# Four units of W1: the low words brought down by ACT and added by POOL, where DVE shifted and merged them

## The chip, the core and the metric

The kernel runs on one core of one Trainium2 chip. The core has five engines with a queue each: TensorE (PE, matmuls, and PEld for its weight loads), VectorE (DVE), ScalarE (ACT), GpSimd (POOL) and SyncE (SP, which here issues the DMAs). Instructions of one engine run in the order of its queue, and wait for others by semaphores. The metric is the device time of one execution in microseconds, lower is better.

## The reference, cut to what matters

```python
def _attn_ref(q, k, v, phi):                    # 8 batches, 8 heads, 576 tokens, 64 wide, 32 memories
    a = softmax(phi, axis=2)                    # over tokens
    k_m = einsum('bhsm,bhsd->bhmd', a, k)
    v_m = einsum('bhsm,bhsd->bhmd', a, v)
    attn = softmax(q @ k_m.T / sqrt(64))
    return attn @ v_m
def _moe_ref(x, w_ch1, w_ch2):                  # x: 8 x 576 x 512
    u = x + real(fft(fft(x, axis=1), axis=2))
    un = (u - mean(u)) / sqrt(var(u) + 1e-6)    # over the 512
    return u + maximum(un @ w_ch1, 0) @ w_ch2   # 512 -> 2048 -> 512
```

The two weight matrices arrive in double precision, 64 bits an element. The kernel needs them in single precision, and makes that on the chip.

## The kernel before, in words

The 4608 tokens are 36 tiles of 128, two tiles a chunk, 18 chunks. For each batch the attention and the transform are made in the background (`background`), and each chunk goes through the two layers: `ffn1` writes hidden values to PSUM (`ph`), ACT applies ReLU, `ffn2` accumulates into `po`, and `finish` adds `u` and stores. W1 and W2 are cut into eight units each, unit j of W1 holding 256 of the 2048 hidden columns and unit j of W2 the matching rows. In this text "W1 unit 3" is that piece; in the code its key is `"1_3"`, and for W2 `"2_3"`.

Chunk 0 goes through the layers while the weights are still coming in, in single precision (`ffn1_direct`, L675, and `ffn2_direct`, L692). For unit j: `load_stage` (L761) brings 1 MB of 64-bit words into a staging place; `to_f32` makes the single-precision values; `ffn1_direct` uses W1 unit j in two halves, `ph_j_0` and `ph_j_1`, each followed by a ReLU on ACT (L678); `ffn2_direct` uses W2 unit j, again in two halves, each of which needs the ReLU of the same half. `split_w1` (L803 and L808, or L806) then makes the pairs of half-precision values with which all later chunks work. The staging places are few: the load of W1 unit 3 goes to the place of W1 unit 1, unit 4 to that of unit 2, unit 6 to that of unit 4, W2 unit 6 to that of W1 unit 5, W1 unit 7 in two halves (tiles `hring` and `uring`) to that of W2 unit 5. A place is free once the conversion has read it for the last time.

`to_f32` treats a 64-bit word as a high and a low word of 32 bits, side by side in the staging tile. For a unit of 128 x 1024 elements:

- L771, ACT: brings the high word, read as a float, into range and drops its sign.
- L773, DVE: shifts the result left by 3 bits, in place.
- L774, DVE: puts the sign back (two operands, the high words and the result).
- then the upper three bits of the low word are set in. For most units DVE does it in one step (L784: shift the low word right by 29 and OR it into the result). For the units in the list `LP`, all of W2, DVE shifts the low word in place (L779, needs nothing but the load) and POOL adds it to the result (L782).
- L793, ACT: sum of squares, from which the unit's scale is made.

The order in each engine's queue is set at build time by a scheduler that runs the program on its own model of time; it is not the order of the code. So a change to `to_f32` also moves instructions that it doesn't touch. Beside the conversions the queues hold, in this stretch, the last tiles of batch 0 (`pp_t`, `px_t` on PE; L600 on ACT; L603, L617 on DVE) and the start of batch 1: transposes of phi (`pf`, `pl`), DVE's reductions to a maximum (L293 to L297), ACT's exponentials (L301 and L302, four of them), the scaling (L311), transposes back (`pt_e`) and the copies to `et` (L315).

Of the kernel before, what the change touches and what calls it, by code (L numbers as in the profile page):

```python
# [15 lines left out]
AF = mybir.ActivationFunctionType  # L16
ALU = mybir.AluOpType
# [33 lines left out]
UW = UB * DM  # L51
EB = 14
L2 = [2, 4, 6]
LP = ["2_0", "2_2", "2_4", "2_6"]
W1_STAGE = ["w4", "w6", "s1", "w6", "s1", "s2", "s1", "x"]
W2_STAGE = ["b10", "b14", "s2", "b10", "b14", "x", "s2", "s1"]
# [75 lines left out]
def kernel(  # L132
# [10 lines left out]
    nc = tc.nc  # L143
# [56 lines left out]
    def tiny(tag, n, bufs=2):  # L200
        if tag not in rings:
            rings[tag] = [taken[0], 0]
            taken[0] += n * bufs
        o, i = rings[tag]
        rings[tag][1] += 1
        o += i % bufs * n
        assert taken[0] <= 400, taken
        return scratch[:, o : o + n]

    def all_sum(src, n, key, pt=None, c0=0):  # L210

        if pt is None:
            pt = psg.tile([P, 512], F32, tag="g", name=f"as_{key}")
        nc.tensor.matmul(pt[:, c0 : c0 + n], lhsT=ones, rhs=src, start=True, stop=True)
        return pt[:, c0 : c0 + n]
# [548 lines left out]
    def to_f32(stages, dst, key):  # L764

        n = UW // len(stages)
        for i, stage in enumerate(stages):
            wf = stage.rearrange("p (a b) -> p a b", b=2)
            hi, lo = wf[:, :, 1], wf[:, :, 0]
            part = dst[:, n * i : n * (i + 1)]  # L770
            nc.scalar.activation(part, hi.bitcast(F32), AF.Abs, scale=2.0**-112)  # L771
            d = part.bitcast(I32)
            nc.vector.tensor_scalar(out=d, in0=d, scalar1=3, scalar2=None, op0=ALU.logical_shift_left)  # L773
            marks[key] = nc.vector.scalar_tensor_tensor(  # L774
                out=d, in0=hi, scalar=-0x80000000, in1=d, op0=ALU.bitwise_and, op1=ALU.bitwise_or
            )
            lu = lo.bitcast(U32)
            if key in LP:
                marks[key] = nc.vector.tensor_scalar(  # L779
                    out=lu, in0=lu, scalar1=29, scalar2=None, op0=ALU.logical_shift_right  # L780
                )
                nc.gpsimd.tensor_tensor(out=d, in0=lo, in1=d, op=ALU.add)  # L782
            else:
                marks[key] = nc.vector.scalar_tensor_tensor(  # L784
                    out=part.bitcast(U32),
                    in0=lu,
                    scalar=29,
                    in1=part.bitcast(U32),
                    op0=ALU.logical_shift_right,
                    op1=ALU.bitwise_or,  # L790
                )
        sq = tiny("sq", 2, 4)
        marks["sq" + key] = nc.scalar.activation(elt.rearrange("p l c -> p (l c)").bitcast(BF16)[:, :UW], dst, AF.Square, accum_out=sq[:, 0:1])  # L793
        return all_sum(sq[:, 0:1], 1, f"sq_{key}")
# [4 lines left out]
    def split_w1(j):  # L799
# [3 lines left out]
        nc.scalar.activation(w[:, 0], src, AF.Copy, scale=s)  # L803
        if j in L2:
            nc.scalar.activation(src, src, AF.Copy, scale=s)
# [6 lines left out]
    def prepare_w1(j):  # L812

        t = w1_f32(j)
        top = to_f32(parts_w1.pop(j), t, f"1_{j}")
        s = s1[:, j : j + 1]
        norm_scale(s, is1[:, j : j + 1], top, 1, 9, f"w1_{j}")
# [4 lines left out]
    def stage_w2(j):  # L822
        top = to_f32(parts_w2.pop(j), w2_f32(j), f"2_{j}")
        norm_scale(s2[:, j : j + 1], is2[:, j : j + 1], top, 1, 14, f"w2_{j}")
# [8 lines left out]
    def prepare_w2():  # L833
        for j in range(NW):
# [3 lines left out]
            nc.scalar.activation(w[:, :, 0], t, AF.Copy, scale=s)  # L838
            if j in L2:
                nc.scalar.activation(t, t, AF.Copy, scale=s)  # L840
# [221 lines left out]
```

## Time and profile before

| | us |
|---|---|
| median of three runs | 996.77 (996.4 to 997.15) |
| the profiled execution | 996.51 |
| its span | 994.6 |
| PE busy, 0 to 65 | 42.47 of 65 |
| PE busy, 65 to 134 (chunk 0 through the layers) | 64.19 of 69 |
| PE busy, 134 to 210 | 68.87 of 76 |
| PE busy, 210 to the end | 780.24 of 784.6 |

The times are of one execution taken by the hardware profiler. Matmuls are pipelined and their ends are modelled. A row of a timeline merges neighbours in the queue of the same line; `xN` says how many, and the bracket behind it how long the engine stood idle before and what ended that. Rows of DVE overlap by some 0.08 us, since the next instruction starts while the last one writes out.

### The profile page before, as it was taken

The numbers are of one execution on the slowest core, as the hardware profiler recorded it, in microseconds if no ns is written. First come the engines' busy times: TensorE is split into PE (matmuls) and PEld (weight loads), VectorE is DVE, ScalarE is ACT, GpSimd is POOL, SyncE is SP. The second block draws the span as 40 slices with busy tenths as digits, with TensorE's granted clock in tenths as the row PEclk, the third lists the DMA queues.
The fourth block names the chain that finished last, engine by engine and source line by source line (L and its number), as shares of the span: only waits on it lengthen the run. The fifth ranks groups of instructions, "written<-read, shape, count | busy, mean of one in ns | idle before, by whom it ended". The sixth has DMA issues, their size and how long they took to land.

```text
span 994.6 us, 18638 instructions
## 1 busy us (share of the span) xinstructions
PE 955.8 (96%) x7644; PEld 685.8 (69%) x7644; DVE 568.1 (57%) x1287; ACT 456.3 (46%) x913; POOL 228.0 (23%) x249
## 2 busy tenths in 40 slices
PE   5769999899999999999999999999999999999998
PEld 5756678666677777767767767777777777766664
DVE  1689967867655575657532576657745676311111
ACT  2265557586535563655431555456545543411100
POOL 1122235235221241233120032113311241300000
PEclk9979999999999999999999999999999999999999
DMA  9706545064222641384210643164213411210000
GB/s 351 270 1 253 184 152 154 2 138 117 64 43 59 136 98 41 56 153 103 58 22 22 117 120 61 48 119 121 68 43 62 101 19 35 44 39 4 22 22 22
DMA packets 115957, 88.06 MB, mean 89 GB/s; under 512 B 100384, under 2 KB 100384, under 8 KB 113824
## 3 DMA queue, kind: packets, MB, share of 16 engines
q1 hardware_dynamic: 115872, 86.87, 34.6%
q8 instruction: 60, 0.98, 0.4%
q14 instruction: 25, 0.20, 0.1%
HBM read 58.15 MB, written 9.44 MB: 68 GB/s over the span
## 4 chain that ended last, share of the span: by engine, by line
PE 84%; DVE 9%; ACT 2%; DMA 2%; issue 1%; SPq 0%; POOL 0%; DVEq 0%; ACTq 0%; POOLq 0%
PE po L728 34%; PE ph L255 33%; PE pm L255 5%; PE pp_t L255 3%; PE psc L255 2%; PE px_t L255 1%; PE pa L548 1%; PE pv L521 1%; PE po L692 1%; DVE w1t L784 1%; DVE uring L617 1%; DVE w2s L774 1%; DMA et<-elt 1%; DMA uring<-in_w 1%; DMA rawt<-in_raw 1%
## 5 line engine op out<-in xcount | busy, mean ns | idle before, releaser
L255 PE MATMUL ph<-unring,w1t 128*128 128x256 f16 x3264 | 390.3, 273 | 2.4 <-DVE scratch L638 1.4
L728 PE MATMUL po<-w2s,hring 128*128 128x512 f16 x1632 | 381.1, 380 | 3.1 <-ACT w2s L838 1.8
L255 PEld LDWEIGHTS <-w1t 128*128 128x128 f16 x3264 | 316.0, 98 | 66.3 <-issue 2.6
L728 PEld LDWEIGHTS <-hring 128*128 128x128 f16 x1632 | 157.6, 98 | 161.5 <-issue 5.6
L719 DVE SCALAR_TENSOR_TENSOR hring<-ph,hring 128x512 f16<-128x512 f32 x136 | 93.3, 686 | 157.4 <-ACT hring L718 156.9
L718 ACT ACTIVATE hring<-ph 128x512 f16<-128x512 f32 x136 | 80.1, 589 | 167.7 <-PE ph L255 167.6
L456 POOL TENSOR_TENSOR aring<-aring,scratch 128x384 f32<-128x384 f32 x28 | 24.7, 882 | 186.6 <-DVE scratch L454 163.5
L641 POOL TENSOR_TENSOR scratch<-scratch,small 128x1 f32<-128x1 f32 x36 | 23.9, 679 | 165.6 <-DVE scratch L640 152.9
L255 PEld LDWEIGHTS <-stg 128*128 128x128 f16 x1152 | 46.1, 98 | 10.3 <-issue 1.7
L373 POOL TENSOR_TENSOR stg<-rawt,stg 128x640 f16<-128x640 f32 x12 | 17.6, 1464 | 122.4 <-ACT rawt L372 122.4
L662 POOL TENSOR_TENSOR ud<-un,ud 128x1024 f16<-128x1024 f32 x17 | 36.7, 2160 | 33.9 <-ACT ud L661 33.8
L255 PE MATMUL pm<-et,stg 128*128 128x64 f16 (+1 forms) x780 | 39.1, 203 | 2.0 <-DMA et<-elt 2.0
L440 DVE TENSOR_REDUCE scratch<-psc 128x12 f32<-128x384 f32 x32 | 17.8, 556 | 39.2 <-PE psc L255 39.1
L255 PE MATMUL pp_t<-vh,at 128*128 128x255 f16 (+3 forms) x288 | 36.7, 273 | 0.0
L603 DVE SCALAR_TENSOR_TENSOR share<-pp_t,scratch,small 128x257 f32<-128x257 f32 (+1 forms) x48 | 21.0, 479 | 26.6 <-ACT small L600 26.5
L740 DVE SCALAR_TENSOR_TENSOR uring<-po,small,uring 128x512 f32<-128x512 f32 x34 | 24.5, 744 | 19.2 <-PE po L728 19.2
L675 PE MATMUL ph<-unring,w1t 128*128 128x256 f32 x128 | 33.5, 409 | 2.0 <-DVE w1t L784 1.5
L475 ACT CAST aeo<-eo 128x384 f16<-128x384 f32 x30 | 15.3, 510 | 43.9 <-DVE eo L472 43.9
L450 ACT ACTIVATE aring<-aring,scratch 128x384 f32<-128x384 f32 x24 | 14.6, 610 | 45.0 <-DVE aring L449 45.0
L617 DVE SCALAR_TENSOR_TENSOR uring<-px_t,scratch,share 128x256 f32<-128x256 f32 (+1 forms) x80 | 33.9, 476 | 0.2
L692 PE MATMUL po<-w2s,hring 128*128 128x512 f32 x64 | 31.5, 621 | 2.4 <-ACT hring L678 2.4
L675 PEld LDWEIGHTS ph<-unring,w1t 128*128 128x128 f32 x128 | 26.0, 207 | 11.1 <-issue 4.6
(226 smaller groups left out, 1271.9 us busy)
## 6 DMA issues: line engine op xcount, KB each, us to landing
rawt<-in_raw SPq DMA_DIRECT2D x15, 640.0 KB, 5.6
stg<-in_raw SPq DMA_DIRECT2D x15, 640.0 KB, 5.1
out<-uring SPq DMA_DIRECT2D x36, 256.0 KB, 2.1
stg<-in_w SPq DMA_DIRECT2D x7, 1024.0 KB, 5.1
rawt<-in_raw SPq DMA_DIRECT2D x15, 384.0 KB, 3.2
stg<-in_raw SPq DMA_DIRECT2D x15, 384.0 KB, 3.2
phs<-in_raw SPq DMA_DIRECT2D x32, 160.0 KB, 5.2
w2s<-in_w SPq DMA_DIRECT2D x4, 1024.0 KB, 9.6
```

What stands on the lines that cost most here:

```text
L255: m = nc.tensor.matmul(out, lhsT=lhsT, rhs=rhs, start=start, stop=stop)
L456: eng.tensor_tensor(out=a, in0=a, in1=sm.unsqueeze(2).to_broadcast([P, 12, M]), op=ALU.mult)
L603: nc.vector.scalar_tensor_tensor(out=tm[rows, w * NJ : (w + 1) * NJ], in0=pp[rows, :NJ], scalar=beta[rows], in1=qs[rows], op0=ALU.mult, op ...
L617: nc.vector.scalar_tensor_tensor(out=u[rows, hs], in0=px[rows, hs], scalar=igx[rows], in1=tm[rows, w * NJ + half : w * NJ + half + 256], o ...
L641: nc.gpsimd.tensor_tensor(out=rs, in0=rs, in1=half, op=ALU.pow)
L662: marks[f"ul{c}"] = nc.gpsimd.tensor_tensor(out=ud[:, 1], in0=un, in1=ud[:, 0], op=ALU.subtract)
L675: nc.tensor.matmul(ph, lhsT=w[:, k, f * P : (f + 1) * P], rhs=unTs[0][:, k], start=(k == 0), stop=(k == NK - 1))
L692: nc.tensor.matmul(po[t], lhsT=h[:, f, t], rhs=w[:, f], start=(j == 0 and f == 0), stop=(j == NW - 1 and f == UB - 1),)
L718: nc.scalar.activation(h[:, 0], phv, AF.Relu)
L719: nc.vector.scalar_tensor_tensor(out=h[:, 1], in0=phv, scalar=0.0, in1=h[:, 0], op0=ALU.max, op1=ALU.subtract)
L728: nc.tensor.matmul(po[t], lhsT=hs[j][:, lh, f * 2 + t], rhs=w2s[:, j * UB + f, lw, :], start=(j == 0 and f == 0 and i == 0), stop=(j == NW ...
L740: nc.vector.scalar_tensor_tensor(out=u, in0=po[t], scalar=cout if c else 0.5, in1=u, op0=ALU.mult, op1=ALU.add)
```

## The change

A new list `LA` names four units of W1. For them L784 is replaced: an activation on ACT reads the low word as an unsigned integer, multiplies it by 2^-29 and writes it back in place as a signed integer; POOL adds it to the result. W1 unit 7 is staged in two places, so it has two activations and two adds of half the size. Lines behind it move down by 1 to 4.

```diff
 L2 = [2, 4, 6]
+LA = ["1_1", "1_3", "1_5", "1_7"]
 LP = ["2_0", "2_2", "2_4", "2_6"]
...
             lu = lo.bitcast(U32)
-            if key in LP:
+            if key in LA:
+                nc.scalar.activation(lo, lu, AF.Copy, scale=2.0**-29)
+                nc.gpsimd.tensor_tensor(out=d, in0=lo, in1=d, op=ALU.add)
+            elif key in LP:
                 marks[key] = nc.vector.tensor_scalar(
                     out=lu, in0=lu, scalar1=29, scalar2=None, op0=ALU.logical_shift_right
                 )
                 nc.gpsimd.tensor_tensor(out=d, in0=lo, in1=d, op=ALU.add)
             else:
```

The queue of ACT in the middle of the stretch, before. `w1t<-stg` is L771 of W1 unit 6, `ph_j_f` (with a buffer number behind) is half f of unit j, whose ReLU it is, and `phs` are the exponentials of batch 1.

```order
L678 ACTIVATE hring<-ph_3_1_801 128x256
L771 ACTIVATE w1t<-stg 128x1024
L678 ACTIVATE hring<-ph_4_0_875 128x256
L678 ACTIVATE hring<-ph_4_1_881 128x256
L678 ACTIVATE hring<-ph_5_0_958 128x256
L301 ACTIVATE phs,scratch<-pf_0_647,scratch 128x512
L302 ACTIVATE phs,scratch<-pl_646,scratch 128x64
L301 ACTIVATE phs,scratch<-pf_1_654,scratch 128x512
L302 ACTIVATE phs,scratch<-pl_646,scratch 128x64
```

The same place now (lines of the changed kernel: L679 is the ReLU, L772 the old L771, L780 the new activation, L302 and L303 the exponentials; `w1t<-hring` is the first half of W1 unit 7).

```order
L772 ACTIVATE w1t<-stg 128x1024
L679 ACTIVATE hring<-ph_3_1_803 128x256
L679 ACTIVATE hring<-ph_4_0_877 128x256
L772 ACTIVATE w2s<-stg 128x1024
L302 ACTIVATE phs,scratch<-pf_0_648,scratch 128x512
L303 ACTIVATE phs,scratch<-pl_647,scratch 128x64
L302 ACTIVATE phs,scratch<-pf_1_655,scratch 128x512
L303 ACTIVATE phs,scratch<-pl_647,scratch 128x64
L679 ACTIVATE hring<-ph_4_1_883 128x256
L772 ACTIVATE w1t<-hring 128x512
L780 ACTIVATE hring<-hring 128x512
L679 ACTIVATE hring<-ph_5_0_961 128x256
```

The ReLU of `ph_3_1` has moved behind L771 of W1 unit 6, and those of `ph_4_1` and `ph_5_0` behind the exponentials of batch 1.

POOL's queue from the conversion of W2 unit 0 on, before (L641 belongs to the normalization of chunk 1, L662 to its split).

```order
L782 TENSOR_TENSOR w2s<-w2s 128x1024
L782 TENSOR_TENSOR w2s<-stg,w2s 128x1024
L641 TENSOR_TENSOR scratch<-scratch,small 128x1 x2
L662 TENSOR_TENSOR ud<-un,ud 128x1024
L782 TENSOR_TENSOR w2s<-w2s 128x1024
```

And now (L786 is the old L782, L663 the old L662, L781 the new add, here of W1 units 1, 3 and 5).

```order
L786 TENSOR_TENSOR w2s<-w2s 128x1024
L781 TENSOR_TENSOR w1t<-w1t 128x1024
L786 TENSOR_TENSOR w2s<-stg,w2s 128x1024
L781 TENSOR_TENSOR w1t<-w1t 128x1024
L642 TENSOR_TENSOR scratch<-scratch,small 128x1 x2
L781 TENSOR_TENSOR w1t<-stg,w1t 128x1024
L663 TENSOR_TENSOR ud<-un,ud 128x1024
L786 TENSOR_TENSOR w2s<-w2s 128x1024
```

Three adds have come in between the four instructions that stood there, and the two of unit 7 follow at the end of the stretch. On DVE the instructions L784 of the four units are gone; at the place of the third add its queue now has, behind L774 of W1 unit 5, a reciprocal of one column, L773 of W2 unit 4, another such reciprocal and L642, and behind L774 of W1 unit 3 a reciprocal, the two L603 and one L617 of a tile, and then L773 of W2 unit 3.

## Rows read from the trace of the kernel before

**Rows 1.** Page: the span, and busy time of each engine (share of the span, instructions).
```profile
span 994.6 us, 18638 instructions
PE 955.8 (96%) x7644; PEld 685.8 (69%) x7644; DVE 568.1 (57%) x1287; ACT 456.3 (46%) x913; POOL 228.0 (23%) x249
```

**Rows 2.** Windows by stage: length, then busy of PE, PEld, DVE, ACT, POOL.
```profile
65.00:134.00 69.00, 64.19 (x272) 44.62 (x273) 64.86 (x95) 37.45 (x64) 17.90 (x8) 0.92 0.48 167
134.00:210.00 76.00, 68.87 (x574) 55.81 (x574) 54.16 (x160) 53.20 (x102) 27.61 (x31) 0.98 0.42 111
210.00:994.60 784.60, 780.24 (x6561) 546.82 (x6556) 414.94 (x940) 344.56 (x704) 170.81 (x189) 1.00 0.31 67
```

**Rows 3.** Timeline of DVE: start, length, line, operation, out<-in; "..." for rows between.
```profile
77.66 1.21 DVE L784 SCALAR_TENSOR_TENSOR w1t<-w1t 128x1024 uint32<-128x1024 uint32 x1
...
83.46 0.86 DVE L603 SCALAR_TENSOR_TENSOR share<-pp_t,scratch,small 128x257 f32<-128x257 f32 x2
84.25 2.85 DVE L784 SCALAR_TENSOR_TENSOR w1t<-stg,w1t 128x1024 uint32<-128x1024 uint32 x1
...
93.21 1.20 DVE L784 SCALAR_TENSOR_TENSOR w1t<-w1t 128x1024 uint32<-128x1024 uint32 x1
...
106.63 2.54 DVE L774 SCALAR_TENSOR_TENSOR w2s<-w2s 128x1024 int32<-128x1024 int32 x1
...
110.29 3.42 DVE L784 SCALAR_TENSOR_TENSOR w1t<-stg,w1t 128x1024 uint32<-128x1024 uint32 x1
...
115.52 0.68 DVE L784 SCALAR_TENSOR_TENSOR w2s<-hring,w2s 128x512 uint32<-128x512 uint32 x1
...
116.72 0.16 DVE L297 TENSOR_SCALAR scratch<-scratch 128x2 f32<-128x2 f32 x1
```

**Rows 4.** Timeline of POOL, the same columns.
```profile
83.60 2.41 POOL L782 TENSOR_TENSOR w2s<-stg,w2s 128x1024 int32<-128x1024 int32 x1 [9.89 <-DVE scratch L222]
...
105.83 2.26 POOL L662 TENSOR_TENSOR ud<-un,ud 128x1024 f16<-128x1024 f32 x1 [5.27 <-ACT ud L661]
109.31 3.32 POOL L782 TENSOR_TENSOR w2s<-w2s 128x1024 int32<-128x1024 int32 x1 [1.21 <-DVE w2s L774]
```

**Rows 5.** Timeline of ACT, the same columns.
```profile
105.63 0.41 ACT L678 ACTIVATE hring<-ph 128x256 f32<-128x256 f32 x1
108.80 1.16 ACT L771 ACTIVATE w1t<-stg 128x1024 f32<-128x1024 f32 x1 [2.76 <-DMA stg<-in_w]
...
112.34 0.39 ACT L678 ACTIVATE hring<-ph 128x256 f32<-128x256 f32 x1 [2.11 <-PE ph L675]
...
116.91 0.69 ACT L301 ACTIVATE phs<-pf,scratch 128x512 f32<-128x512 f32 x1 [0.67 <-DVE scratch L297]
...
118.74 0.21 ACT L302 ACTIVATION_READ_ACCUMULATOR phs<-pl,scratch 128x1 f32 x1
...
121.89 0.68 ACT L771 ACTIVATE w1t<-hring 128x512 f32<-128x512 f32 x1 [1.77 <-DMA hring<-in_w]
```

**Rows 6.** Timeline of PE, the same columns.
```profile
96.10 3.23 PE L692 MATMUL po<-w2s,hring 128*128 128x512 f32 x4 [1.93 <-ACT hring L678]
99.12 2.35 PE L675 MATMUL ph<-unring,w1t 128*128 128x256 f32 x8
...
105.19 1.88 PE L692 MATMUL po<-w2s,hring 128*128 128x512 f32 x4
...
110.35 1.89 PE L675 MATMUL ph<-unring,w1t 128*128 128x256 f32 x8
113.77 1.99 PE L675 MATMUL ph<-unring,w1t 128*128 128x256 f32 x8 [1.53 <-DVE w1t L784]
115.60 3.60 PE L692 MATMUL po<-w2s,hring 128*128 128x512 f32 x8
```

**Rows 7.** Windows around two waits of PE; granted clock is the figure after POOL's.
```profile
98.00:100.00 2.00, 2.00 (x5) 1.04 (x4) 2.00 (x3) 0.17 (x1) 2.00 (x1) 0.50 0.66 266
112.00:114.00 2.00, 0.47 (x3) 0.23 (x2) 2.00 (x2) 0.39 (x1) 0.63 (x1) 1.00 0.00 0
```

## The prediction

> **What bounds the kernel now.** I read the page first, then the windows by stage, then the timelines of DVE, POOL, ACT and PE from 65 to 134 us. The page gives a span of 994.6 us with TensorE busy for 96% of it [rows 1]; the profiled execution took 996.51 us, so 1.9 us lie around the span, and it stands 0.26 us under the median of 996.77. The windows say where the remaining 4% are [rows 2]. From 210 us on, PE is busy for 780.24 of 784.6 us: nothing there waits for the other engines, and whatever PE has lost by then stays lost. From 65 to 134 us, where units of W1 and W2 are converted and used at once, DVE is busy for 64.86 of 69 us and PE for 64.19. So DVE has no reserve exactly where this change works, PE has 4.8 us of idle time, ACT (37.45) and POOL (17.90) have room. That is the case for the change. The timelines decide whether it holds.
>
> **What goes.** For W1 units 1, 3, 5 and 7, DVE's last conversion step (L784) goes: 1.21 us for unit 1, 1.20 for unit 3, and 3.42 for unit 5, of which 1.2 is its own work [rows 3]. Unit 7 comes in two halves of about 0.68 each, as the half of W2 unit 5 shows [rows 3]. DVE's own work falls by 3 x 1.2 + 2 x 0.68 = 5.0 us.
>
> **What comes on ACT.** One activation per unit. The trace has none from uint32 to int32; the nearest row is the activation of the same 1024 strided words at L771, 1.16 us [rows 5]. Bounds: 0.7 us (the same line's half of 512 words, 0.68 [rows 5]) and 2.3 us, twice the row, as a wide end. I take 1.16, the nearest row: 4.6 us in all, in a stretch where ACT is idle for 31 us. It is in ACT's queue ahead of the first ReLU and makes that 1.1 us later; PE has 1.93 us of waiting at 96.10 and 1.53 at 113.77 further on [rows 6] in which this disappears, so I count it at nothing. At 2.3 us it would still be under the sum of the two.
>
> **What comes on POOL, and what that does to DVE.** Five integer adds, four of 1024 words in work. Before has four such adds for W2: the one at 83.60 took 2.41 us, the one at 109.31 took 3.32, the other two lie between [rows 4]. The end of a DVE instruction that meets one is telling: the add of 83.60 ended at 86.01, and the L784 started at 84.25 ended at 87.10, 1.09 after it, about its own length, though 2.85 long [rows 3, 4]. The same at 110.29: the add ends at 112.63, L784 1.08 later, 3.42 long [rows 3, 4]. So an instruction of DVE with both operands in SBUF stands still until the add is through: 1.64 and 2.21 us lost. The two L603 that read PSUM ran in 0.86 us beside the add of 83.60 [rows 3]. The price of an add to DVE lies therefore between 0 (only PSUM readers beside it) and 2.3 us (the add without its own waiting: 112.63 less 110.3, where it could begin).
>
> The rule that speaks against this change is in the Trainium skill, "SBUF — State Buffer", section "Who interferes with whom": the port pair that VectorE and GpSimd share is a lock, held for a whole instruction, and the loser stops. The rows above agree. By the rule alone three full locks would cost 7.0 us where I count 5.55 below, and the forecast would be 1.4 us higher.
>
> In the new queue of DVE the add of unit 1 meets L773 and L774 of the next units (SBUF only): 2.2. That of unit 3 meets the two L603 and one L617 first (PSUM, 1.2 us), then stops L773: 1.15. That of unit 5 meets tiny ones and then L642 (SBUF): 2.2. Sum 5.55 us, against two removed L784 (units 1 and 3, 2.4 us) ahead of the same place, the L774 of W2 unit 4. Two POOL instructions that before has too fall on other instructions of DVE: the add of W2 unit 2 now stops L773 for some 2.1 us where it stopped L784 for 1.64, and L662, which stretched L774 at 106.63 to 2.54 (1.33 lost [rows 3, 4]), comes nearer to its start: +0.5 each. DVE is late there by 5.55 - 2.4 + 1.0 = 4.1 us. The next add (W2 unit 4) costs 2.2 as before, on another instruction, and L784 of unit 5 (1.2) is gone from behind it: +2.9 us at L297, which started at 116.72 [rows 3]. It now starts at 119.6.
>
> **Why PE feels it.** Before, ACT ran the ReLU of ph_4_1 (L678, 112.34) ahead of the four exponentials of the next batch (116.91 to 118.95), which wait for L297 [rows 5]. In the new order the four stand in front of that ReLU. They start at 119.6 + 0.2, end at 121.8, the ReLU ends near 122.3. The second half of po for unit 4 needs it: before it began at 115.60 + 1.75 = 117.35, half of the eight matmuls of 3.60 us [rows 6]. It now begins near 122.4: **+5.0 us**. PE's queue between is ph_4_1, ph_5_0 and the first half of po, which needs the add of W2 unit 4 (4.1 us later than 112.63, so 116.8): done by 118.7. PE then waits for 3.7 us with nothing to fill it.
>
> Another ReLU, that of ph_3_1, ran at 105.63 ahead of the L771 of unit 6, which waited for its load until 108.80 [rows 5]. It now stands behind that L771, so po of unit 3 is some 3 us late as well; but ph_5_0, the one matmul that waited for L784 of unit 5 (1.53 us [rows 6]), has its unit early now. Both are over before 118 and are swallowed by the wait above, so neither is in the sum.
>
> After such a wait the clock falls. After the wait of 1.93 us at 96.10 the granted clock was 0.50 (the 1.2 GHz level) in 98 to 100, four L692 took 3.23 us where 1.88 is usual and eight L675 took 2.35 where 1.89 is usual: 1.8 us [rows 6, 7]. After the wait of 1.53 at 113.77 it stayed at 1.00 and nothing was lost [rows 6, 7]. For 3.7 us I count **+1.8 us**. The ReLU of ph_5_0 comes behind the load of unit 7's first half (5.7 us from the L784 that frees its place, ending at 116.20, to L771 at 121.89 [rows 3, 5]), L771 and the new activation: 116.20 + 2.9 + 5.7 + 1.3 = 126.1, ReLU done at 126.5, while PE at full clock would want it at 125.9. At half clock PE arrives later still, so this wait of 0.6 lies inside the 1.8.
>
> From 134 to 210 us PE is idle for 7.1 of 76 us [rows 2]. The chain there starts from PE's own results, so it moves along; DVE however is late by less than PE (3 against 7), and may hand back a little: I take **-0.3**. Sum: 5.0 + 1.8 - 0.3 = 6.5; 996.51 + 6.5 = 1003.0 us, and against the median the same within 0.3.
>
> **The rivals.**
> Faster: the locks cost nothing since most instructions beside the new adds would be PSUM readers. For it: L603 in 0.86 us [rows 3]. Then L297 comes at 116.72 - 3.6 = 113.1, the exponentials are over at 115.3, no ReLU waits, and unit 5 is ready some 3.5 us earlier; PE gains its 1.53 and some of the 1.93 with the clock behind it, bounded by the 3.5 by which DVE is early: 993 us. It decides at about 1.2 us per add; below that DVE gains. Against it: in the queue the adds of units 1 and 5 meet SBUF instructions.
> No change: the 7 us are lost at 122 and given back in the 7.1 us that PE idles between 134 and 210 [rows 2], because ACT and DVE get ahead: 997 us. Against it: that stretch starts from matmuls on PE that are themselves late.
> Slower still: the wait of ph_3_1 also drops the clock (1.8), ACT's new operation takes 2.3 us and sits in front of the ReLU of ph_5_0 and of the batch's exponentials' scaling (+1.2): 1006 to 1009 us.
>
> **How the numbers follow.** Forecast 0.70, with its own range 999 to 1006 (the lock sum between 1.4 less and the full 7.0, with or without the clock's 1.8). Faster 0.08, no change 0.13, slower still 0.09. About 0.2%, 2 us, is what a measurement of this kernel can tell from no change. Hence faster 0.08, same 0.13, slower 0.79. The range goes from 997.0, which takes in about half of the no-change case, to 1007.0, which takes in the lower part of the slowest; about 2 in 10 lie outside.
>
> **What would show it.** Right: DVE instructions of 2.5 to 3.4 us behind the new adds of units 1 and 5; L297 between 119 and 121 us; the ReLU of ph_4_1 behind the four exponentials, ending near 122; a wait of PE of 3 to 4 us before the second half of po for unit 4, released by ACT, and a clock of 0.5 just after it; PE's idle time after 210 as small as before. Wrong: L297 at or before 116.7 (the locks don't cost), no wait of PE near 120 (ACT's order doesn't matter), or PE idle for less than 3 us from 134 to 210 (given back).

## The result, and the profile after

The changed kernel took 1003.84 us (median of 3, 1003.29 to 1004.36) where the kernel before took 996.77; the ratio is 1.0071 with a 95% interval of 1.0048 to 1.0094, slower. The forecast was 1003.0. The profiled execution has a span of 1002.0 us against 994.6 [rows 1].

On the chips of the experiments the executions of nearly every kernel fall into two groups some 8 to 11 us apart, because all that follows the start-up stands that much earlier in one of them (first matmul of the two layers at 59 or at 68 us); the medians below are of the later group, in which both kernels above lie, while the ratios and intervals hold both groups and shift with a kernel's share of each (e4 has none of the earlier group, e8 half, the kernel before about a third).

The three stages after the change, in the columns of [rows 2]:

```profile
65.00:134.00 69.00, 58.19 (x239) 39.54 (x240) 65.31 (x88) 40.53 (x67) 26.60 (x13) 0.93 0.46 160
134.00:210.00 76.00, 70.37 (x557) 56.78 (x556) 52.44 (x156) 48.80 (x95) 23.54 (x27) 0.98 0.39 105
210.00:1002.00 792.00, 785.23 (x6606) 550.03 (x6603) 421.37 (x946) 349.34 (x713) 174.73 (x192) 1.00 0.31 68
```

DVE, from which work was taken, is no less busy (65.31 us against 64.86): what went came back as standing still. PE is idle for 10.81 us of the first stage where it was idle for 4.81. Line numbers after the change are higher by 1 (by 4 behind the new lines L780, ACT, and L781, POOL).

POOL's timeline (start, length, line, operation), with the new adds of units 1, 3 and 5, answers to [rows 4]:

```profile
75.12 2.73 POOL L781 TENSOR_TENSOR w1t<-w1t 128x1024 int32<-128x1024 int32 x1 [1.22 <-ACT w2s L772]
...
90.10 2.40 POOL L781 TENSOR_TENSOR w1t<-w1t 128x1024 int32<-128x1024 int32 x1 [1.95 <-ACT w2s L772]
...
106.25 2.70 POOL L781 TENSOR_TENSOR w1t<-stg,w1t 128x1024 int32<-128x1024 int32 x1 [2.81 <-DVE small L234]
```

DVE's timeline beside them answers to [rows 3]:

```profile
74.91 0.68 DVE L774 TENSOR_SCALAR w2s<-w2s 128x1024 int32<-128x1024 int32 x1
75.52 2.89 DVE L774 TENSOR_SCALAR w1t<-w1t 128x1024 int32<-128x1024 int32 x1
...
91.12 1.93 DVE L774 TENSOR_SCALAR w2s<-w2s 128x1024 int32<-128x1024 int32 x1
...
106.68 2.55 DVE L643 TENSOR_SCALAR un<-uring,scratch 128x512 f32<-128x512 f32 x1
...
120.01 0.16 DVE L298 TENSOR_SCALAR scratch<-scratch 128x2 f32<-128x2 f32 x1
```

Each of these three adds has one DVE instruction beside it that is long by the rest of the add: L774, 0.68 us when alone, took 2.89 and 1.93; L643, 0.53 alone, took 2.55. L298 starts at 120.01 where L297 started at 116.72 [rows 3].

ACT's timeline, as [rows 5]: the ReLU of ph_3_1 (the first of the two merged ones) behind L772 of W1 unit 6 and L662, which waits for the long L643 of DVE; then the first exponential of the next batch, the end of the fourth, and the ReLU of ph_4_1 behind them.

```profile
109.27 1.05 ACT L662 CAST ud<-un 128x1024 f16<-128x1024 f32 x1 [1.99 <-DVE un L643]
110.22 1.12 ACT L772 ACTIVATE w1t<-stg 128x1024 f32<-128x1024 f32 x1
111.24 0.64 ACT L679 ACTIVATE hring<-ph 128x256 f32<-128x256 f32 x2
...
120.20 0.69 ACT L302 ACTIVATE phs<-pf,scratch 128x512 f32<-128x512 f32 x1 [1.93 <-DVE scratch L298]
...
122.02 0.21 ACT L303 ACTIVATION_READ_ACCUMULATOR phs<-pl,scratch 128x1 f32 x1
122.12 0.39 ACT L679 ACTIVATE hring<-ph 128x256 f32<-128x256 f32 x1
```

PE's timeline, as [rows 6]; the number in brackets is the wait ahead of the row and what ended it:

```profile
111.66 3.33 PE L693 MATMUL po<-w2s,hring 128*128 128x512 f32 x4 [1.95 <-ACT hring L679]
114.79 4.01 PE L676 MATMUL ph<-unring,w1t 128*128 128x256 f32 x16
118.63 1.88 PE L693 MATMUL po<-w2s,hring 128*128 128x512 f32 x4
122.56 1.98 PE L693 MATMUL po<-w2s,hring 128*128 128x512 f32 x4 [2.06 <-ACT hring L679]
...
131.38 1.98 PE L693 MATMUL po<-w2s,hring 128*128 128x512 f32 x4 [0.65 <-ACT hring L679]
...
215.21 1.03 PE L256 MATMUL pm<-et,stg 128*128 128x64 f16 x30 [1.29 <-DMA et<-elt]
...
231.56 0.81 PE L729 MATMUL po<-w2s,hring 128*128 128x512 f16 x3 [0.26 <-DVE w2s L847]
...
239.21 2.32 PE L729 MATMUL po<-w2s,hring 128*128 128x512 f16 x10 [0.67 <-POOL w2s L845]
```

The matmul at 215.21 is this one of the kernel before:

```profile
209.43 1.03 PE L255 MATMUL pm<-et,stg 128*128 128x64 f16 x30 [1.53 <-DMA et<-elt]
```

PE is 0.2 us late already at 67.9 (68.08 against 67.88), 5.2 us at 122.56 (117.35 before, by the prediction's working), 5.8 at 215.21, and 7.4 at the end.

### The profile page after: what moved, and what is told of

The parts are those of the page before. It is cut to its first block, busy times and chain, and to the rows that moved or that the text cites. A ratio compares the mean times of both kernels' runs of the same rounds, so it can differ in the third digit from the quotient of the medians.

```text
span 1002.0 us, 18650 instructions
## 1 busy us (share of the span) xinstructions
PE 956.9 (95%) x7644; PEld 685.0 (68%) x7644; DVE 573.1 (57%) x1282; ACT 459.8 (46%) x918; POOL 236.3 (24%) x254
## 4 chain that ended last, share of the span: by engine, by line
PE 81%; DVE 10%; ACT 3%; issue 2%; DMA 1%; POOL 1%; SPq 0%; DVEq 0%; ACTq 0%; POOLq 0%
PE po L729 33%; PE ph L256 32%; PE pm L256 5%; PE pp_t L256 3%; PE psc L256 2%; PE px_t L256 1%; PE pa L549 1%; DVE w2s L775 1%; PE pv L522 1%; PE po L693 1%; DVE uring L618 1%; DVE un L643 1%; DVE w1t L775 1%; DVE w2s L774 1%; DMA rawt<-in_raw 1%
## 5 line engine op out<-in xcount | busy, mean ns | idle before, releaser
L642 POOL TENSOR_TENSOR scratch<-scratch,small 128x1 f32<-128x1 f32 x36 | 21.1, 589 | 169.0 <-DVE scratch L641 156.3
L663 POOL TENSOR_TENSOR ud<-un,ud 128x1024 f16<-128x1024 f32 x17 | 36.6, 2152 | 30.0 <-ACT ud L662 29.9
L465 POOL TENSOR_TENSOR ahring<-aring,ahring 128x320 f16<-128x320 f32 x29 | 24.0, 827 | 38.8 <-ACT ahring L464 38.7
```

Of the source, the lines that this page charges most:

```text
L465: nc.gpsimd.tensor_tensor(out=ahl[:, :, 64:128], in0=av[:, 0:5], in1=ahl[:, :, 0:64], op=ALU.subtract)
L642: nc.gpsimd.tensor_tensor(out=rs, in0=rs, in1=half, op=ALU.pow)
L663: marks[f"ul{c}"] = nc.gpsimd.tensor_tensor(out=ud[:, 1], in0=un, in1=ud[:, 0], op=ALU.subtract)
```

## The experiments

Idle time of PE by stage (length of the window less busy, in us; for the two kernels whose profiled execution began earlier, e9 and e12, the windows are 8.6 us earlier), and the median beside that of the kernel before on the same chip:

| kernel | 65 to 134 | 134 to 210 | 210 to 290 | median | before | ratio (95%) |
|---|---|---|---|---|---|---|
| before | 4.81 | 7.13 | 0.00 | | | |
| after | 10.81 | 5.63 | 2.46 | 1003.84 | 996.77 | 1.0071 (1.0048 to 1.0094) |
| e1 ACT scales, DVE merges | 8.13 | 6.23 | 2.35 | 1001.52 | 996.27 | 1.0050 (1.0013 to 1.0086) |
| e2 DVE shifts, POOL adds | 9.27 | 5.19 | 1.56 | 1001.24 | 996.27 | 1.0066 (1.0024 to 1.0109) |
| e3 no add | 6.78 | 4.97 | 0.00 | 993.88 | 996.27 | 0.9976 (0.9939 to 1.0013) |
| e4 unit 7 alone | 5.82 | 6.46 | 0.02 | 997.19 | 996.27 | 1.0054 (1.0020 to 1.0088) |
| e5 add aside | 11.01 | 5.28 | 2.33 | 1003.59 | 996.57 | 1.0069 (1.0030 to 1.0107) |
| e6 exponentials late | 9.04 | 5.61 | 1.47 | 1003.20 | 996.57 | 1.0038 (1.0003 to 1.0074) |
| e7 as e1, other form | 7.43 | 5.45 | 2.33 | 1001.14 | 996.57 | 1.0045 (1.0003 to 1.0087) |
| e8 short adds | 7.17 | 4.83 | 0.00 | 997.97 | 996.57 | 0.9986 (0.9941 to 1.0032) |
| e9 ReLUs first | 10.49 | 6.05 | 2.43 | 1005.21 | 996.75 | 1.0070 (1.0030 to 1.0110) |
| e10 as e1, W2 unit 4 on DVE | 4.81 | 9.65 | 0.56 | 1000.33 | 996.75 | 1.0051 (1.0014 to 1.0089) |
| e11 before without POOL adds | 8.57 | 5.27 | 0.00 | 997.77 | 996.75 | 1.0007 (0.9974 to 1.0040) |
| e12 e11, L662 on DVE | 2.87 | 9.90 | 0.00 | 995.78 | 995.91 | 0.9968 (0.9929 to 1.0008) |

**Is it the lock?** Three kernels: without the add, with the add but nobody waiting for it, with a short add.

e3, the merge left out for the four units of W1:

```diff
                 nc.scalar.activation(lo, lu, AF.Copy, scale=2.0**-29)
-                nc.gpsimd.tensor_tensor(out=d, in0=lo, in1=d, op=ALU.add)
```

> Leaves out the merge of the low three bits for W1 units 1, 3, 5 and 7: ACT scales the low words as in the changed kernel, and neither POOL nor DVE adds them. ACT's queue again has the four exponentials in front of the second ReLU of unit 4, as in the changed kernel. Theory L: without the locks and without L784 DVE is some 4 to 5 us earlier at L298 than before (112 to 114), the exponentials stand before the ReLU and cost nothing there, and the time is 992 to 996. Rival A (ACT's activations cost): 1001 to 1004. Rival O (it is the order in ACT's queue that costs, whether DVE is locked or not): PE waits some 2 us before the second half of unit 4's po, 999 to 1003.

Measured 993.88, 10 us under the changed kernel and 2.4 under the one before (the interval holds no change): the lock theory's range. L298 starts 2.8 us earlier than before, counted from the first matmul of the two layers. ACT's work is that of the changed kernel, and the exponentials stand in front of the ReLU of ph_4_1 here too, where PE waits 1.67 us: neither costs 7 us by itself.

e5, the sum written to the staging area; no instruction changes its place in any queue:

```diff
-                nc.gpsimd.tensor_tensor(out=d, in0=lo, in1=d, op=ALU.add)
+                nc.gpsimd.tensor_tensor(out=lo, in0=lo, in1=d, op=ALU.add)
```

> The changed kernel with one operand changed: each new add on POOL writes its sum over the scaled low words in the staging area and not into the unit, so the low three bits of W1 units 1, 3, 5 and 7 are left out of the result. Every engine's queue has the same order as in the changed kernel, POOL adds as long and locks DVE as before; only nobody who uses the unit waits for the add. Theory L (the lock on DVE is the cost): nearly all of the loss stays, 1001 to 1004, with the wait of PE before the second half of unit 4's po as in the changed kernel. Rival W (the unit is ready later, since an add takes 2.4 us on POOL where L784 took 1.2 on DVE): the loss goes, 994 to 997.

Measured 1003.59, the loss of the changed kernel, with PE's wait for the same ReLU (PE's timeline of e5):

```profile
121.51 3.68 PE L693 MATMUL po<-w2s,hring 128*128 128x512 f32 x4 [3.47 <-ACT hring L679]
```

No user of a unit waits for an add here, and the locks are there: L774 takes 2.90 and 1.93, and a third instruction, L775, 2.62 where 1.21 is usual. L298 starts at 118.95, 2.6 us later than before, counted in the same way (3.1 in the changed kernel). The staging places are not it either: the adds are through with those of units 1, 3 and 5 at 77.31, 91.96 and 109.58, where L784 was at 78.87, 94.41 and 113.71. So it is what the adds do to DVE, and not that a unit or a place is ready later; between these two this run decides.

e8, the adds cut to 64 words:

```diff
-                nc.gpsimd.tensor_tensor(out=d, in0=lo, in1=d, op=ALU.add)
+                nc.gpsimd.tensor_tensor(out=d[:, :64], in0=lo[:, :64], in1=d[:, :64], op=ALU.add)
```

> The changed kernel with the new adds on POOL cut to the first 64 of 1024 words of each unit (64 of 512 for the halves of unit 7); the other low bits are left out of the result. The four exponentials again stand in front of the second ReLU of unit 4 on ACT, and ACT's work is the same. The add is short: it locks DVE for some 0.2 us. Theory L: 991 to 996, like the kernel without the add. Rival O (the order of the queues is what costs): 1000 to 1004.

Measured 997.97, above the range of the lock theory by 2 and below the rival's: most of the loss goes with the length of the add, and L298 starts 3.5 us earlier than before, counted in the same way. Part of what DVE gains is lost on PE before 118.58, where it waits for the ReLU of ph_4_1, which here stands on ACT behind the exponentials and also behind W1 unit 7's first activation (PE's timeline of e8):

```profile
118.58 3.78 PE L693 MATMUL po<-w2s,hring 128*128 128x512 f32 x4 [3.48 <-ACT hring L679]
```

That wait is one of order, not of the lock. No run takes the lock away and keeps every queue of the changed kernel as it is: e3 and e8 both differ from it in a few places.

**Which half?** e1, ACT scales and DVE merges:

```diff
-                nc.gpsimd.tensor_tensor(out=d, in0=lo, in1=d, op=ALU.add)
+                marks[key] = nc.vector.tensor_tensor(out=d, in0=lo, in1=d, op=ALU.bitwise_or)
```

> Half of the change: for W1 units 1, 3, 5 and 7 ACT scales the low words down as in the changed kernel, but DVE merges them (a tensor_tensor OR of about 1.2 us in place of L784), so POOL gets nothing new. Theory L (the POOL adds lock DVE out of SBUF, L298 is 3 us late, the exponentials stand before the second ReLU of unit 4 on ACT, PE waits): without the adds no lock is new, L298 starts within 1 us of 116.7, and the time is that of before within 2 us: 995 to 999. Rival A (the four activations of 1.14 us in ACT's queue make the ReLUs late): the ACT load is the same as in the changed kernel, so most of the loss stays: 1001 to 1004.

Measured 1001.52: the lock theory's number is wrong and the rival's right. PE's longest wait from 70 to 134 us, though, is for POOL and not for a ReLU. POOL's timeline, then DVE's from its start to its end, then PE's:

```profile
108.77 8.66 POOL L786 TENSOR_TENSOR w2s<-w2s 128x1024 int32<-128x1024 int32 x1 [2.36 <-ACT w1t L772]
```

```profile
108.48 1.27 DVE L812 SCALAR_TENSOR_TENSOR w1t<-w1t,small 128x1024 f16<-128x1024 f32 x1
109.67 1.21 DVE L781 TENSOR_TENSOR w1t<-stg,w1t 128x1024 int32<-128x1024 int32 x1
...
113.96 1.21 DVE L775 SCALAR_TENSOR_TENSOR w1t<-stg,w1t 128x1024 int32<-128x1024 int32 x1
115.83 2.15 DVE L783 TENSOR_SCALAR stg<-stg 128x1024 uint32<-128x1024 uint32 x1 [0.67 <-DMA stg<-in_w]
```

```profile
117.48 5.40 PE L693 MATMUL po<-w2s,hring 128*128 128x512 f32 x8 [4.55 <-POOL w2s L786]
```

Here the lock falls the other way round. POOL's add of W2 unit 4, which the kernel before has too (3.32 us [rows 4]), stands still while L812 ends and nine further instructions of DVE pass at their usual lengths (L781 to L775 above, back to back); it gets in at the first gap of DVE, 115.17, ends 2.3 us later, and DVE's next instruction waits for it.

e2, the other half:

```diff
-LA = ["1_1", "1_3", "1_5", "1_7"]
-LP = ["2_0", "2_2", "2_4", "2_6"]
+LA = []
+LP = ["1_1", "1_3", "1_5", "1_7", "2_0", "2_2", "2_4", "2_6"]
```

> The other half: units 1, 3, 5 and 7 go the way that W2 units 0, 2, 4 and 6 go already, DVE shifts and POOL adds; ACT gets nothing new. Theory L: the locks of the changed kernel (2.2, 1.15, 2.2 us and their like) are all there, and DVE keeps a shift per unit besides (0.6 to 1.2 us each): L298 is at 120 or later, PE waits for the second ReLU of unit 4, 1002 to 1007. Rival A (ACT's activations): nothing on ACT, so 996 to 998.

Measured 1001.24, 0.8 below the range and 3 above the rival's. With nothing new on ACT most of the loss is there, and L298 starts at 120.32, as the lock theory said. But DVE keeps a shift per unit here, and PE waits for two adds themselves, besides 1.59 us for the ReLU of ph_4_1, so this run does not separate the lock from units that are ready later:

```profile
115.29 2.00 PE L676 MATMUL ph<-unring,w1t 128*128 128x256 f32 x8 [1.18 <-POOL w1t L786]
...
119.30 1.99 PE L693 MATMUL po<-w2s,hring 128*128 128x512 f32 x4 [2.02 <-POOL w2s L786]
```

e7 asks whether the form of DVE's instruction keeps POOL out:

```diff
-                marks[key] = nc.vector.tensor_tensor(out=d, in0=lo, in1=d, op=ALU.bitwise_or)
+                marks[key] = nc.vector.scalar_tensor_tensor(
+                    out=d, in0=lo, scalar=0, in1=d, op0=ALU.logical_shift_right, op1=ALU.bitwise_or
+                )
```

> As the ACT-and-DVE half, but DVE merges by a scalar_tensor_tensor (shift by 0, then OR), the form of L788, and not by a tensor_tensor; the queues have the same order. With the tensor_tensor POOL's add of W2 unit 4 took 8.66 us, from 108.77 to 117.43, while DVE ran without a gap at its usual lengths, and PE waited 4.55 us for it. Theory F (the form of the DVE instruction decides whether POOL gets in at its end): the add takes 3 to 4 us, 996 to 998. Rival G (POOL gets in only at a gap in DVE's work or beside an instruction that reads PSUM, whatever the form): the add takes over 7 us again, 1001 to 1002.

Measured 1001.14, the rival's number, and the add takes 8.66 us again, PE waits 4.55 again: between these two forms there is no difference.

e10 takes the starved add away from e1:

```diff
-LP = ["2_0", "2_2", "2_4", "2_6"]
+LP = ["2_0", "2_2", "2_6"]
```

> The ACT-and-DVE half, with W2 unit 4 merged by DVE as well (LP without 2_4), so the POOL add that took 8.66 us and held PE for 4.55 us is not there. Theory P (that half lost its 5 us to this one starved add on POOL): 994 to 997.5. Rival A (ACT's activations of 1.14 us cost, the add only happened to be waited for): 1000 to 1002.

Measured 1000.33, the rival's number: 3.6 us over before, where e1 is 5.2 over. Yet the wait of 4.55 us is gone, and PE's idle time from 65 to 134 us is that of the kernel before, 4.81: ACT's activations cost nothing there on balance. Some 3 us are lost later, with no new add on POOL: from 134 to 210 us 9.65 idle against 7.13, and 0.56 against 0.00 behind it. Why the order chosen for that stage loses them was not tried, so 3.6 us of loss without a new lock stay without a cause.

**How does DVE's lateness reach PE?** e6 holds the four exponentials behind the ReLU of ph_4_1 (cut; ex and ey name the exponentials; line numbers behind this place are higher by 7 than in the changed kernel):

```diff
+            r = nc.scalar.activation(h[:, f], ph, AF.Relu)
+        if j == 4:
+            for e in ("ex1_0", "ey1_0", "ex1_1", "ey1_1"):
+                tc.add_manual_dep(marks[e].ins, r.ins.name, ...)
```

> The changed kernel with the four exponentials of the next batch held behind the second ReLU of unit 4 in ACT's queue, as they stand before the change (issue order alone, no wait). The prediction put 5.0 us on their standing in front. By that term: 998 to 1000. By the trace of the changed kernel, in which PE waited 2.06 us for that ReLU: the 2.06 goes and a part comes back at the next ReLU, 1001 to 1003. Rival: the place does not matter, DVE's lateness reaches PE by other ways: 1003 to 1005.

Measured 1003.20: the rival, by 0.2. ACT's and PE's timelines show where the wait went:

```profile
122.99 0.67 ACT L779 ACTIVATE w1t<-hring 128x512 f32<-128x512 f32 x1 [1.37 <-DMA hring<-in_w]
123.57 0.69 ACT L787 ACTIVATE hring<-hring 128x512 int32<-128x512 uint32 x1
124.16 0.36 ACT L679 ACTIVATE hring<-ph 128x256 f32<-128x256 f32 x1
```

```profile
124.57 3.55 PE L700 MATMUL po<-w2s,hring 128*128 128x512 f32 x4 [2.65 <-ACT hring L679]
```

PE runs through unit 4's po without a wait and stops at the next ReLU, that of ph_5_0: ahead of it on ACT is W1 unit 7, whose load goes to a place that DVE frees late (first half at 118.87, before at 116.20). Behind 2.65 us of waiting the four matmuls take 3.55 us instead of 1.88, at half clock.

e9 moves both behind the ReLU of ph_5_0: the edge of e6 at unit 5's first ReLU, and in `GATE1`, which names what the preparation of a W1 unit is held behind, that ReLU (`r5_0`) for unit 7:

```diff
-GATE1 = [[]] + [["un1", "uh0"]] * 7
+GATE1 = [[]] + [["un1", "uh0"]] * 6 + [["un1", "r5_0"]]
```

> The changed kernel, all its POOL adds kept, with both things that stood in front of a ReLU on ACT put behind the first ReLU of unit 5: the four exponentials (they wait for DVE's L298) and the activations of W1 unit 7 (they wait for a load whose place DVE frees late). Holding back the exponentials alone moved PE's wait from 122.56 (2.06 us) to 124.57 (2.65 us) and gained nothing. Theory Q (DVE's lateness reaches PE through ACT's queue, by whatever stands ahead of the ReLU): with both gone PE runs on from 120 to about 124, and 3 to 5 us come back: 998.5 to 1001. Rival R (the next unit, converted late by DVE, stops PE anyway): 1002 to 1004.

Measured 1005.21, above both ranges (the runs of the median lie between 1001.94 and 1009.83). Nothing comes back; the wait has gone on to the ReLU of ph_5_1, behind the activation of W2 unit 7 that waits for its load (ACT, then PE; this execution stands some 9 us earlier):

```profile
121.03 1.12 ACT L779 ACTIVATE w2s<-stg 128x1024 f32<-128x1024 f32 x1 [2.95 <-DMA stg<-in_w]
122.06 0.64 ACT L679 ACTIVATE hring<-ph 128x256 f32<-128x256 f32 x2
```

```profile
122.48 3.29 PE L700 MATMUL po<-w2s,hring 128*128 128x512 f32 x4 [3.69 <-ACT hring L679]
```

That load goes to the place of W1 unit 6 and is issued when DVE is through with it, 2.8 us later than before, counted from the first matmul of the two layers. Three kernels, three different ReLUs, much the same loss (7.1, 6.6 and 8.5 us). The place on ACT picks the ReLU, not the size.

e4, the change for unit 7 alone:

```diff
-LA = ["1_1", "1_3", "1_5", "1_7"]
+LA = ["1_7"]
```

> The changed way for W1 unit 7 alone, whose two half adds on POOL come at about 128 us, after L298; ACT's queue has the second ReLU of unit 4 in front of the exponentials, as before. Theory L: the adds of units 1, 3 and 5 are what counts, so the start of L298 and the PE wait near 122 are as before, and the two half locks (1 us each) fall in a stretch where the next PE wait is released by others: 995.5 to 998. Rival S (each of the four adds takes its share of the 7 us wherever it stands): 998 to 999.5.

Measured 997.19, as theory L had it. Of the 0.9 over before the row below shows most: PE waits 1.19 us where it waited 0.17, for L312 on ACT, which stands behind two new half activations of 0.67 each. Here ACT's share is not nothing, though the load ahead of them also came some 0.4 us later.

```profile
125.78 0.66 PE L315 MATMUL pt_e<-identf,phs 128*128 128x128 f32 x4 [1.19 <-ACT phs L312]
```

**The change turned round.** e11, the kernel before without its own four adds on POOL:

```diff
-LP = ["2_0", "2_2", "2_4", "2_6"]
+LP = []
```

> The kernel before with its own four POOL adds taken back as well (W2 units 0, 2, 4 and 6 merged by DVE like the others): the change turned round. Before, these adds stretched DVE's instructions at 71.6, 84.25, 110.29 and 124.69 by 2.1, 1.6, 2.2 and 2.2 us, 8.1 in all, and saved DVE 4 x (1.21 - 0.69) = 2.1 us of its own work. Theory L: DVE is 6 us earlier by 125 us, PE's waits of 1.93 and 1.53 shrink, with them the half clock that follows the first: 992 to 995.5. Rival O (the new order of the queues brings new waits of the same size): 995.5 to 999.

Measured 997.77, the number of rival O, with an interval that holds no change. L297 starts at 105.83, 11 us earlier, and PE runs from 76 to 119 us without a wait. Then it loses it all at once. POOL, SP's queue (SPq), ACT and PE:

```profile
103.83 11.89 POOL L662 TENSOR_TENSOR ud<-un,ud 128x1024 f16<-128x1024 f32 x1 [5.95 <-ACT ud L661]
```

```profile
115.75 1.87 SPq L238 DMA_TRANSPOSE unring<-ud  x1
117.73 1.06 SPq L761 DMA_DIRECT2D stg<-in_w  x1
```

```profile
123.61 1.12 ACT L771 ACTIVATE w2s<-stg 128x1024 f32<-128x1024 f32 x1 [10.86 <-DMA stg<-in_w]
```

```profile
125.44 1.11 PE L314 MATMUL pt_e<-identf,phs 128*128 128x128 f32 x4 [6.30 <-ACT phs L311]
```

DVE has no gap until 113.8, POOL's subtraction is held until then, the transposing DMA that needs it holds SP's queue, and behind it is the load of W2 unit 6. e12 is e11 with that subtraction given to DVE:

```diff
-        marks[f"ul{c}"] = nc.gpsimd.tensor_tensor(out=ud[:, 1], in0=un, in1=ud[:, 0], op=ALU.subtract)
+        marks[f"ul{c}"] = (nc.vector if c == 1 else nc.gpsimd).tensor_tensor(out=ud[:, 1], in0=un, in1=ud[:, 0], op=ALU.subtract)
```

> The kernel before with its four POOL adds taken back and POOL's subtraction for the next chunk (L662, 1024 words) given to DVE too, so that POOL has no long operation from 65 to 125 us. With the adds alone taken back PE ran from 76 to 119 us without a wait; then L662, starved on POOL by an unbroken DVE (11.89 us, 103.83 to 115.72), held the transposing DMA and behind it on SP's queue the load of W2 unit 6, ACT and DVE stood 10.9 us, and PE waited 6.30 us. Theory P (that one starved POOL operation ate what the locks had given back): L662 costs DVE 1.3 us, the load comes some 9 us earlier, PE's wait goes or falls under 1 us: 989 to 993. Rival D (the loads of the last units come too late in any case, since their places come free late): PE waits 3 to 6 us at another place, 994 to 998.

Measured 995.78 (before 995.91), rival D's number; the interval ends at 1.0008, so a gain is not shown. L662 takes 1.23 us on DVE, PE's 6.30 are gone (2.13 stand at another ReLU), and its idle time in the first stage falls to 2.87. Two of the windows of e12, moved to its earlier start, and two waits of PE in the second:

```profile
56.40:125.40 69.00, 66.13 (x283) 46.26 (x283) 58.36 (x95) 37.74 (x65) 2.19 (x2) 0.94 0.54 183
125.40:201.40 76.00, 66.10 (x547) 53.30 (x546) 52.21 (x161) 54.33 (x103) 28.16 (x31) 0.98 0.43 98
```

```profile
167.59 2.58 PE L255 MATMUL ph<-unring,w1t 128*128 128x256 f16 x22 [2.14 <-POOL w1t L806]
...
193.98 7.08 PE L255 MATMUL ph<-unring,w1t 128*128 128x256 f16 x48 [3.08 <-DMA unring<-ud]
```

The stage behind it is idle for 9.90 us where 7.13 were: PE comes earlier and waits for W1's halves from POOL and for the transposed chunk. No kernel here is shown to beat the one before.

## Why the prediction was right

**What goes and what ACT pays.** L780 took 1.13 to 1.16 us for a unit (1.16 taken) and 0.69 and 0.68 for the halves of unit 7, 4.8 in all where 4.6 was taken. That it costs nothing holds on balance in e10's first stage and not in e4, where it costs up to 1.0.

**The locks.** Unit 1 lost 2.89 - 0.68 = 2.2 us (2.2 predicted), unit 3 1.93 - 0.68 = 1.25 (1.15), unit 5 2.55 - 0.53 = 2.0 (2.2): 5.5 against 5.55, on the kinds of instruction that were named. L298 came at 120.01, 119.6 predicted. e3, e5 and e8 show them to be the cause of DVE's lateness and of most of the loss: it leaves with the adds or with their length and stays when nobody waits for them. What part of the 7 us is the new order's, apart from the locks, is open: e10 loses 3.6 us with no new add.

**Plus 5.0 before the second half of po.** It began at 122.56, 122.4 predicted, 5.2 late. The way there is where the prediction failed. It said that PE would come at 118.7 and wait 3.7 us, with the wait for the ReLU of ph_3_1 over and swallowed. PE waited 1.95 there, ran its next matmuls at half clock (3.33 us for four), came at 120.5 and waited 2.06. That first ReLU was late not only by the load ahead of it, as the prediction had it: L772 of W1 unit 6 began at 110.22 (108.80 before) behind L662, which waited for the DVE instruction that the third add had stopped. And the exponentials in front of the ReLU of ph_4_1 are not what makes the 5.0: with them behind it (e6) the same loss appears one ReLU on, and with W1 unit 7 out of the way too (e9), one further. DVE's lateness reaches PE by whichever entry of ACT's queue hangs on DVE.

**Plus 1.8 of clock.** Not at its place: after 122.56 four matmuls took 1.98 us. The half clock came behind the wait at 111.66, and what it cost there was covered by the next wait: e5, at full clock there (four matmuls in 1.98 us), waits 3.47 where the changed kernel waits 2.06, and loses as much. Windows behind both waits after the change; the third figure from the end is the granted clock, 0.53 and 1.00, so the 1.2 GHz level nearly throughout and then the 2.4 GHz level:

```profile
112.00:114.50 2.50, 2.50 (x4) 1.01 (x3) 2.50 (x2) 0.00 (x0) 1.34 (x2) 0.53 0.74 246
122.60:124.40 1.80, 1.80 (x5) 0.84 (x6) 1.80 (x3) 0.93 (x2) 0.00 (x0) 1.00 0.78 319
```

**Minus 0.3 from 134 to 210.** Nothing was handed back on balance; PE is 5.8 late at 215.21 as it was at 134.92 (129.14 before).

**What was missing:** some 1.6 us behind 210. There the new order of PE's queue uses W2's f16 pairs sooner than they are made (0.26 and 0.67 in the rows above); the window from 210 to 290 has 2.46 us of idle time, of which 1.29 stand before 215.21, so 1.17 are found. The other 0.4 was not located. By the spans the sum is 7.4 us, made of 5.2, 0.6 for the wait at 131.38 and 1.6, where the prediction had 5.0, 1.8 and -0.3: the total was near because one miss stood in for another.

**The rivals.** "Faster" and "no change" are out by the medians. That the second stage evens out the first is what happens to a gain, though: in e12 PE idles 1.9 us less than before up to 134 and 2.8 more after, and in e10 3.3 less than in e1 and then 3.4 more. "Slower still" had the ReLU of ph_3_1 and its clock right and the price wrong, since the later wait covers them.

## What to carry to other kernels

In this kernel, work moved from VectorE to GpSimd was not off VectorE while both worked on SBUF: look up which VectorE instructions will stand beside the GpSimd one in the new queue, and charge what is left of it where they read SBUF (1.25 to 2.2 us an add here), or else the GpSimd one's own lateness, as in e1. Test such a cause by keeping the operation and taking away only its users, as e5 does, before going after the wait that it shows up as; moving that wait's neighbours (e6, e9) only moved the wait. And a stage with one late engine has many outlets: count the lateness of that engine, not the waits one by one.

## What was not expected of the hardware

In the contest of DVE and POOL for SBUF, POOL can be shut out for long: its instruction took 8.66 us in e1 and e7 and 11.89 in e11, while nine and more DVE instructions behind one another each ran at their usual length, until DVE had a gap. In the kernels before and after, POOL's add got in between two such instructions about 1 us after its start (109.31 and 3.32 long [rows 4]). The Trainium skill, "SBUF — State Buffer", section "Who interferes with whom", says that whoever issues first gets the shared port pair for the whole instruction and the other is blocked. Read so, the add of e1 would have begun at 109.75, when L812 ended. It did not, and the measurement decides. What makes the one or the other win at a boundary these runs do not show.

TensorE's granted clock after a wait is not told by the length of the wait alone: behind 1.95 us at 111.66 it was 0.53 and four matmuls took 3.33 us after the change; behind the same 1.95 us in e6, at the same ReLU, it was 1.00 and they took 1.98. Windows of e6 behind that wait, and behind the one of 2.65 us:

```profile
111.10:112.80 1.70, 1.70 (x4) 0.80 (x5) 1.70 (x1) 0.16 (x1) 0.80 (x1) 1.00 0.85 357
124.70:127.70 3.00, 3.00 (x4) 1.38 (x5) 3.00 (x4) 1.02 (x3) 2.25 (x2) 0.50 0.79 320
```
